# Seven block products for eight in the first products of three experts

## The chip, the cores and the metric

The kernel runs on one core of a Trainium2 chip. The engines of that core are TensorE (PE in the profile; PEld is its weight load), VectorE (DVE), ScalarE (ACT), GpSimd (POOL) and the queue engine SyncE (SP), which starts the DMA transfers. SBUF is the core's main memory, PSUM the memory of eight banks into which TensorE writes its sums. The metric is the time of one execution on the device, in microseconds (us): the median of three runs.

## The reference

Three networks follow each other on 1152 tokens (2 batches of 576) of 512 features.

```python
# attention: 8 heads of 64, a window of 128 keys back, a bias per head
scores = where(mask, scale * q @ k.T + bias, -1e9); attn = softmax(scores); x = attn @ v
# network one: four experts, F = 1024
p = domain_probs / domain_probs.sum(-1)
for e in range(4):
    out += p[:, e:e+1] * (maximum(x @ w1[e], 0) @ w2[e])
# network two, F = 2048
h = maximum(x @ w_in, 0);  y = (h * h) @ w_out
```

## The kernel before

**Three products for one.** Each fp32 operand is kept as a rounded high part and the rest (names that end in h and l). A product is three matmuls into one sum: high by high, and high by rest both ways.

**Items.** Network two is cut into two halves of 1024 hidden columns, which count as experts 4 and 5 (E = 4 is the number of real experts, NE = 6 of both). The tokens of an expert are cut into three chunks of 384 (CHUNKS); expert 0, which runs beside the attention, has four chunks (256, 256, 256, 384: CHUNKS0). An item (e, ch, f) is a chunk and one of the eight tiles of 128 hidden columns. Its first product (gemm1_mm, matmuls on L757) sums over four tiles of 128 features: 4 x 3 = 12 matmuls of 384 columns into one "work" bank. ScalarE writes the relu's high part (hh, L772), VectorE the rest (hl, L773); in network two VectorE squares first (L779) and POOL writes the rest (L781). The second product (gemm2, L791) is 3 token tiles x 3 = 9 matmuls of 512 columns into three "y" banks, and runs LAG = 3 items behind. After the eighth f of a chunk VectorE adds the three y banks to y in SBUF, times the expert's probability (L805 for expert 0, L809 for experts 1 to 3).

**Weights.** They come in quarters g of 256 hidden columns: a w1 tile of 128 x 4 x 256 and a w2 tile of 128 x 2 x 512. For experts 1 to 3 ScalarE writes the high part (L273) and POOL the rest (L275). The weights of network two come as 64-bit floats that VectorE takes apart in integer steps (split64: L199, L202, L206, L210, and the rest L275), with ScalarE copies between (L195, L273).

**What sets the order.** A planner (Plan, with costs and due times) orders the attention together with expert 0's first three chunks. From expert 0's last chunk on (item N1 = 24) a loop at the end of the function writes the items out one after another. Each engine runs its instructions in the order in which that loop issues them. Small closures prepare the weights of what comes later; pace gives each item its number of them. Between experts 3 and 4, y is turned into the x of network two by TensorE transpositions (to_x2, L823, four of 128 x 128 for each token tile), with the high part on ScalarE (L827) and the rest on VectorE (L828); one token tile every second item.

Of the kernel before, what the change touches and what calls it, by code (L numbers as in the profile page):

```python
# [10 lines left out]
I32 = mybir.dt.int32  # L11
# [12 lines left out]
CHUNKS = [(0, 384), (384, 384), (768, 384)]  # L24

# [103 lines left out]
def kernel(  # L129
# [34 lines left out]
    hp = ctx.enter_context(tc.tile_pool(name="hp", bufs=4))  # L164
# [17 lines left out]
    def split64(raw, n, t):  # L182

        lo, hi = raw[:, :, 0], raw[:, :, 1]
        stt = nc.vector.scalar_tensor_tensor

        def begin():
            t["a"] = late["w"].tile([P, n], F32, tag="wfull", name="wfull", bufs=3)
            t["b"] = late["w"].tile([P, n], I32, tag="wtmp", name="wtmp", bufs=2)
            t["ai"] = t["a"].bitcast(I32)
            nc.scalar.activation(out=t["a"], in_=hi.bitcast(F32), func=ACTF.Abs, scale=65536.0)  # L195

        return [
            begin,
            lambda: nc.vector.tensor_scalar(  # L199
                out=t["b"], in0=hi, scalar1=-(1 << 31), scalar2=None, op0=ALU.bitwise_and  # L200
            ),
            lambda: nc.vector.tensor_scalar(  # L202
                out=t["a"], in0=t["a"], scalar1=8053063680.0, scalar2=2.0,
                op0=ALU.min, op1=ALU.max,
            ),
            lambda: stt(  # L206
                out=t["b"], in0=lo, scalar=29, in1=t["b"],
                op0=ALU.logical_shift_right, op1=ALU.bitwise_or,
            ),
            lambda: stt(  # L210
                out=t["ai"], in0=t["ai"], scalar=3, in1=t["b"],
                op0=ALU.logical_shift_left, op1=ALU.bitwise_or,
            ),
        ]
# [10 lines left out]
    free = []  # L225
    raws = {}
# [31 lines left out]

    def w_ops(i):
# [4 lines left out]
        parts = (w1t, w2t)[k]  # L264

# [50 lines left out]
    def chunks(e):  # L316
# [4 lines left out]
        rq=3, rk=3, rv=2, qh=2, ql=2, khl=2, vp=2, sc=2, tp=2, ts=5, st=5, pt=2, work=2, y=2, h=4  # L321
# [440 lines left out]

    def h_tiles(n):
        return [hp.tile([P, 3 * P], F32R, tag=t, name=t)[:, 0:n] for t in ("hh", "hl")]

    def gemm1(e, ch, f):
# [9 lines left out]
        else:  # L776
            r = late["w"].tile([P, n], F32, tag="r", name="r", bufs=2)
# [18 lines left out]
    def evac(e, ch, tiles):  # L796
        c0, cn = chunks(e)[ch]
# [21 lines left out]
    def to_x2(ch, i):  # L819
        nt = CHUNKS[ch][0] // P + i  # L820
# [23 lines left out]
    items = [(e, ch, f) for e in range(NE) for ch in range(len(chunks(e))) for f in range(FT)]  # L844
    first_item = [items.index((e, 0, 0)) for e in range(NE)]
# [6 lines left out]
    def run_x2():  # L852
        if x2todo:
            what = x2todo.pop(0)
            if what:
                to_x2(*what)

    def flush_one():
        e, ch, f, h = pend.pop(0)
        if f == 0:  # L860
            ys[e, ch] = [
                (i, ps_tile("y", [P, DM], "yacc")) for i in range(chunks(e)[ch][1] // P)
            ]
        gemm2(e, ch, f, h, ys[e, ch])
        w_done(w2t, e, ch, f)
        if f == FT - 1:
            evac(e, ch, ys.pop((e, ch)))
            if e == E - 1:
                x2todo.extend(x for i in range(CHUNKS[ch][1] // P) for x in (None, (ch, i)))

    def attn_close():
        if "w" not in late:
            actx.close()
            late["w"] = ctx.enter_context(tc.tile_pool(name="wlate", bufs=1))
            add_buffers(late["w"], 12)
# [4 lines left out]
    def loads(limit=len(order), ahead=2 * NQ):  # L880

        while wnext["load"] < limit:
            i = wnext["load"]
            wait = i - wnext["ops"] + bool(bg)
            wide = order[i][0] >= E
            if wait >= ahead or (wide and "w" not in late):
                return
            narrow = sum(order[p][0] < E for p in range(i - wait, i))
            if len(free) < 2 + narrow + (2 if wide else 1):
                return  # L890
            w_load(i)
            wnext["load"] += 1

    def pace(it):

        i = wnext["ops"]
        if i == len(order):
            return len(bg)
        pe = order[i][0]
        if pe == 0:  # L900
            return 1
        left = max(first_item[pe] - it - 1, 1)
        todo = ((pe + 1) * PER - i) * (1 if pe < E else 14) + len(bg)
        return -(-todo // left)

    def bg_some(n):
        for _ in range(n):
            if not bg and wnext["ops"] < wnext["load"]:
                w_start()
            bg_run(1)  # L910

    def w_done(parts, e, ch, f):
        if ch == len(chunks(e)) - 1 and f % FTQ == FTQ - 1:
# [190 lines left out]
    attn_close()  # L1104

    for it, (e, ch, f) in list(enumerate(items))[N1:]:
        loads()
        need = 2 * (e * NQ + f // FTQ) + 1
        if need not in ready:
            bg_run()  # L1110
            while wnext["ops"] <= need:
                loads()
                w_start()
                bg_run()
            while carry:
                carry.pop(0)()
        run_x2()
        quota = pace(it)
        pend.append((e, ch, f, gemm1(e, ch, f)))
        w_done(w1t, e, ch, f)  # L1120
        bg_some(quota - quota // 2)
        if len(pend) > LAG:
            flush_one()
        bg_some(quota // 2)

# [37 lines left out]
```

## Time and profile before

| | us |
|---|---|
| median of three runs | 703.45 (703.31 to 703.74) |
| the profiled execution | 703.92, of which the span is 702.1 |
| TensorE busy | 691.1 |
| VectorE busy | 301.7 |
| ScalarE busy | 260.8 |
| POOL busy | 204.7 |

Busy times are sums over a group's instructions; matmuls overlap in their pipeline, so the spacing of starts, not the duration of one, says what a matmul costs in a row. The chain is followed back from the last instruction to what released it; a piece of it on TensorE is time in which nothing else held the program.

### The profile page before, as it was taken

How to read it: one execution, taken by the hardware profiler on the slowest of the kernel's cores; microseconds unless marked ns; L12 is line 12 of the kernel's file. 1: busy time of each engine (PE TensorE's matmuls, PEld its weight loads, DVE VectorE, ACT ScalarE, POOL GpSimd, SP SyncE). 2: the span in 40 equal slices, each digit the busy share in tenths (PEclk: the TensorE clock that was granted, in tenths of full speed). 3: DMA queues.
4: the chain of work that ended last, by engine and by line, in shares of the span. 5: the costliest groups of instructions: out<-in, count | busy, mean ns of one | idle time of the engine just before them, and what ended most of it. 6: DMA issues, size and time to landing. Idle time of an engine off the chain costs nothing.

```text
span 702.1 us, 9945 instructions
## 1 busy us (share of the span) xinstructions
PE 691.1 (98%) x3848; PEld 624.1 (89%) x3848; DVE 301.7 (43%) x706; ACT 260.8 (37%) x601; POOL 204.7 (29%) x212
## 2 busy tenths in 40 slices
PE   8998999999999999999999999999999999999997
PEld 7787998889999999999999999999999999999996
DVE  4688867732121212122123656527776627112121
ACT  5886777533331113311112222314445434322221
POOL 4898745408550004510011000000222222222221
PEclk7899999999999999999999999999999999999999
DMA  8753221233400011300005400036300020001011
GB/s 211 204 165 91 79 73 44 71 104 107 150 31 1 0 31 61 119 31 1 0 31 186 175 0 1 31 122 212 117 0 1 31 91 0 1 1 45 1 46 45
DMA packets 37103, 47.58 MB, mean 68 GB/s; under 512 B 3392, under 2 KB 25408, under 8 KB 37056
## 3 DMA queue, kind: packets, MB, share of 16 engines
q1 hardware_dynamic: 37056, 46.95, 21.5%
q8 instruction: 30, 0.49, 0.3%
q14 instruction: 17, 0.14, 0.1%
HBM read 44.58 MB, written 2.36 MB: 67 GB/s over the span
## 4 chain that ended last, share of the span: by engine, by line
PE 91%; POOL 1%; issue 0%; DVE 0%
PE yacc L791 42%; PE hps L757 42%; PE xps L578 3%; PE tp L680 2%; PE sc L632 1%; PE xtp L823 1%; POOL vl L349 0%; POOL ql L349 0%; POOL wl L349 0%; POOL ts L668 0%; DVE y L815 0%
## 5 line engine op out<-in xcount | busy, mean ns | idle before, releaser
L757 PE MATMUL hps<-xh,wh 128*128 128x384 f32 (+1 forms) x608 | 202.1, 332 | 0.6 <-DVE hl L1062 0.6
L757 PE MATMUL hps<-xh,wl 128*128 128x384 f32 (+1 forms) x608 | 200.2, 329 | 0.0
L757 PE MATMUL hps<-xl,wh 128*128 128x384 f32 (+1 forms) x608 | 199.7, 328 | 0.0
L791 PE MATMUL yacc<-wh,hl 128*128 128x512 f32 x432 | 170.8, 395 | 0.0
L791 PE MATMUL yacc<-wl,hh 128*128 128x512 f32 x432 | 170.5, 395 | 0.0
L791 PE MATMUL yacc<-wh,hh 128*128 128x512 f32 x432 | 169.2, 392 | 0.0
L773 DVE SCALAR_TENSOR_TENSOR hl<-hps,hh 128x384 fp32r<-128x384 f32 x80 | 44.6, 557 | 227.7 <-ACT hh L772 227.6
L772 ACT ACTIVATE hh<-hps 128x384 fp32r<-128x384 f32 x80 | 39.4, 492 | 245.1 <-PE hps L757 245.1
L781 POOL TENSOR_TENSOR hl<-r,hh 128x384 fp32r<-128x384 f32 x48 | 50.8, 1058 | 266.0 <-ACT hh L780 262.5
L757 PEld LDWEIGHTS hps<-xh,wh 128*128 128x128 f32 x608 | 115.3, 190 | 6.7 <-DVE hl L1062 0.8
L757 PEld LDWEIGHTS hps<-xl,wh 128*128 128x128 f32 x608 | 115.2, 189 | 5.3
L757 PEld LDWEIGHTS hps<-xh,wl 128*128 128x128 f32 x608 | 114.9, 189 | 0.0
L275 POOL TENSOR_TENSOR wl<-wraw,wh 128x1024 fp32r<-128x1024 f32 x24 | 57.2, 2390 | 173.0 <-ACT wh L273 165.7
L791 PEld LDWEIGHTS yacc<-wh,hl 128*128 128x128 f32 x432 | 81.0, 187 | 17.5
L791 PEld LDWEIGHTS yacc<-wl,hh 128*128 128x128 f32 x432 | 81.1, 188 | 13.3
L791 PEld LDWEIGHTS yacc<-wh,hh 128*128 128x128 f32 x432 | 81.2, 188 | 12.8
L779 DVE TENSOR_TENSOR r<-hps,r 128x384 f32<-128x384 f32 x48 | 26.7, 556 | 102.6 <-ACT r L778 102.6
L778 ACT ACTIVATE r<-hps 128x384 f32<-128x384 f32 x48 | 23.6, 491 | 92.0 <-PE hps L757 92.0
L668 POOL TENSOR_SCALAR ts<-ts,st 128x256 f32<-128x256 f32 (+2 forms) x80 | 38.8, 498 | 33.4 <-DVE st L663 18.5
L653 ACT ACTIVATE ts<-ts,st 128x256 f32<-128x256 f32 (+2 forms) x80 | 37.1, 466 | 9.0 <-DVE st L644 8.9
L780 ACT ACTIVATE hh<-r 128x384 fp32r<-128x384 f32 x48 | 25.2, 526 | 35.6 <-DVE r L779 35.6
L275 DVE TENSOR_TENSOR wl<-wfull,wh 128x512 fp32r<-128x512 f32 x32 | 28.3, 884 | 6.4 <-ACT wh L273 6.4
(76 smaller groups left out, 686.5 us busy)
## 6 DMA issues: line engine op xcount, KB each, us to landing
wraw<-in_w_dram SPq DMA_DIRECT2D x32, 512.0 KB, 3.8
wraw<-in_w_in_dram SPq DMA_DIRECT2D x16, 512.0 KB, 4.3
wraw<-in_w_out_dram SPq DMA_DIRECT2D x16, 512.0 KB, 4.2
rq<-in_qT_dram SPq DMA_DIRECT2D x8, 256.0 KB, 6.7
out_dram<-y SPq DMA_DIRECT2D x8, 256.0 KB, 2.1
rk<-in_kT_dram SPq DMA_DIRECT2D x8, 192.0 KB, 6.6
rv<-in_v_dram SPq DMA_DIRECT2D x8, 192.0 KB, 2.6
rq<-in_qT_dram SPq DMA_DIRECT2D x8, 192.0 KB, 2.5
```

Of the source, the lines that this page charges most:

```text
L275: eng.tensor_tensor(out=lo[:, ks, :], in0=full, in1=f32(hi[:, ks, :]), op=ALU.subtract)
L578: nc.tensor.matmul(out=xps[0:rows, o0:o0 + w], lhsT=l_, rhs=r_, start=start, stop=(i == len(mm) - 1 and a == 0 and l_ is wl_), skip_group_ ...
L653: nc.scalar.activation(out=ts[0:n, g, :], in_=ts[0:n, g, :], func=ACTF.Exp, bias=st[0:n, 0, g:g + 1], scale=-1.0, accum_out=st[0:n, 1, g:g ...
L668: nc.gpsimd.tensor_scalar(out=ts[0:n, g, :], in0=ts[0:n, g, :], scalar1=st[0:n, 2, g:g + 1], scalar2=1.0, op0=ALU.mult, op1=ALU.mult,)
L757: nc.tensor.matmul(out=ps, lhsT=l_[:, k, cs], rhs=r_[:, k, cols], start=(k == 0 and r_ is xh and l_ is wh and not second), stop=(k == KT - ...
L772: nc.scalar.activation(out=hh, in_=ps, func=ACTF.Relu)
L773: nc.vector.scalar_tensor_tensor(out=hl, in0=ps, scalar=0.0, in1=f32(hh), op0=ALU.max, op1=ALU.subtract)
L778: nc.scalar.activation(out=r, in_=ps, func=ACTF.Relu)
L779: nc.vector.tensor_tensor(out=r, in0=ps, in1=r, op=ALU.mult)
L780: nc.scalar.activation(out=hh, in_=r, func=ACTF.Copy)
L781: nc.gpsimd.tensor_tensor(out=hl, in0=r, in1=f32(hh), op=ALU.subtract)
L791: nc.tensor.matmul(out=y, lhsT=l_[:, ns], rhs=r_[:, fo, :], start=(f == 0 and j == 0), stop=(f == FT - 1 and j == 2),)
```

## The change

**Seven products.** For experts 1 to 3 the tokens are cut into pairs of two equal halves: pair A is tokens 0 to 511 (2 x 256), pair B tokens 512 to 1151 (2 x 320). With the 512 features in two halves and a quarter's 256 hidden columns in two halves, the first product of a pair and a quarter is a 2 x 2 by 2 x 2 block product, and seven block products with sums of blocks (Winograd's form) take the place of eight. The item is now (e, pair, quarter): 7 products x 2 feature tiles x 3 = 42 matmuls (gemm1_pair, L891) of 256 or 320 columns, into three banks pa, pb, pc. In the order of the code the seven are a11·b11 (pa), s2·t2 (pb), s1·t1 (pc), a12·b21 (on top in pa), s3·t3 (on top in pb, after VectorE has read u2 = pb + p1), s4·b22 (on top in pc, after ScalarE has copied p5), a22·m4 (on top in pb, after u3 = pb + p1). VectorE makes the sums u2, u3, c12, c21 and the four rests hl, ScalarE the copies p1, p5 and the four high parts, POOL c22.

**Sums of weights.** For each quarter POOL forms the four sums s1 to s4 (wsum, four adds, L281) and the rests la and ls (L402); ScalarE the high parts ha (L287) and hs (L306). These closures stand in w_forms.

**Sums of x.** VectorE forms t1, t2, m4 and t3 for each pair, high part and rest (x_forms, adds on L846, ScalarE copies on L864), in six steps. The loop issues pair A's steps behind the first six items of expert 0's last chunk, and pair B's three behind each of the first two paired items. Expert 1's items come in the order (A, quarter 0), (A, 1), (B, 0), (B, 1), (A, 2), (A, 3), (B, 2), (B, 3), as for the other two.

**Second products.** gemm2_pair (L940) is 4 or 5 token tiles x 2 x 3 matmuls of 512 columns, one item behind. y is added after every two quarters (L989): 54 adds for 27.

**Into network two.** The transpositions (now L1002, with xh on ScalarE and xl on VectorE, L1007) of pair A's four token tiles stand right behind the first products of the last paired item; the other five are spread over every second item as before. The buffers for weights are cut anew (18 + 6, and 8 more once network two begins), rk of the attention has two slots for three, and loads, pace and the look-ahead are rewritten to go by time.

```diff
+PAIRS = [(0, 256), (512, 320)]
...
+        return [
+            begin,
+            lambda: (part(0, 4, raw[:, :, 0:P]), part(4, 2, a22)),
+            lambda: add(0, lambda: a21, lambda: a22, ALU.add),
+            lambda: add(2, s(0), lambda: a11, ALU.subtract),
+            lambda: add(4, lambda: a11, lambda: a21, ALU.subtract),
+            lambda: add(6, lambda: a12, s(2), ALU.subtract),
+            lambda: part_lo(0, 4, raw[:, :, 0:P]),
+            lambda: (part_lo(4, 2, a22), free.append(buf)),
+            lambda: nc.scalar.activation(out=t["hs"][0], in_=t["s"], func=ACTF.Copy),
+            done,
+        ]
...
-        rq=3, rk=3, rv=2, qh=2, ql=2, khl=2, vp=2, sc=2, tp=2, ts=5, st=5, pt=2, work=2, y=2, h=4
+        rq=3, rk=2, rv=2, qh=2, ql=2, khl=2, vp=2, sc=2, tp=2, ts=5, st=5, pt=2, work=2, y=2, h=4
...
+        t1 = make(0, "t1", ((h12, h11), ((l12, plus), (l11, sub))))
+        t2 = make(1, "t2", ((h22, lambda: place(0)), ((l22, plus),)))
+        m4 = make(0, "m4", ((h21, lambda: place(1)), ((l21, plus),)))
+        t3 = make(1, "t3", ((h22, h12), ((l22, plus), (l12, sub))))
+        return [
+            t1[0], t1[1] + t2[0], t1[2] + t2[1] + m4[0], t2[2] + m4[1] + t3[0], m4[2] + t3[1],
+            t3[2],
+        ]
...
+        pa, pb, pc = (ps_tile("work", [P, n], "hps") for _ in range(3))
+        mm(pa, a11, f["b11"], True, False)
+        nc.scalar.activation(out=p1, in_=pa, func=ACTF.Copy)
+        mm(pb, s2, f["t2"], True, False)
+        add(u2, pb, p1)
+        mm(pc, s1, f["t1"], True, False)
+        nc.scalar.activation(out=p5, in_=pc, func=ACTF.Copy)
+        mm(pa, a12, f["b21"], False, True)
+        relu(0, 0, pa)
+        mm(pb, s3, f["t3"], False, False)
+        add(u3, pb, p1)
+        mm(pc, s4, f["b22"], False, True)
+        add(c12, pc, u2)
+        relu(0, 1, c12)
+        mm(pb, a22, f["m4"], False, True)
+        add(c21, pb, p1)
+        relu(1, 0, c21)
+        nc.gpsimd.tensor_tensor(out=c22, in0=u3, in1=p5, op=ALU.add)
+        relu(1, 1, c22)
...
+    xbg = x_forms(0, "DVE") + [[]] * 2 + x_forms(1, "DVE")
...
         quota = pace(it)
-        pend.append((e, ch, f, gemm1(e, ch, f)))
+        if paired(e):
+            h = gemm1_pair(e, ch, f)
+            if it == items.index((E, 0, 0)) - 1:
+                run_x2(4)
+                x2wait = it + 2
...
         w_done(w1t, e, ch, f)
+        x_step()
+        if paired(e):
+            x_step()
         bg_some(quota - quota // 2)
-        if len(pend) > LAG:
+        if len(pend) > (1 if paired(e) else LAG):
             flush_one()
+        if paired(e):
+            x_step()
         bg_some(quota // 2)
```

How the instructions stand on three engines, before and now. First VectorE where expert 1 begins: in the kernel before, the rests hl (L773) of items and the y adds of chunks.

```order
L773 SCALAR_TENSOR_TENSOR hl<-hps,hh 128x384 x3
L805 TENSOR_SCALAR y<-yacc,pt 128x512 x2
L773 SCALAR_TENSOR_TENSOR hl<-hps,hh 128x384 x8
L805 TENSOR_SCALAR y<-yacc,pt 128x512 x3
L773 SCALAR_TENSOR_TENSOR hl<-hps,hh 128x384 x8
```

The same place in the changed kernel, from the last rest of item (1, A, 0) to the sums of item (1, A, 1); fxwork is the work tile of x_forms, lt the rest of t1, u and c the sums of the seven products (L901).

```order
380 L906 SCALAR_TENSOR_TENSOR hmem<-c_2542,hmem 128x256
381 L985 TENSOR_SCALAR y<-yacc,pt 128x512 x3
382 L846 TENSOR_TENSOR fxwork<-xh 128x640
383 L846 TENSOR_TENSOR fxwork<-fxwork,xl 128x640 x2
384 L846 TENSOR_TENSOR fxwork<-xh,fxwork 128x640
385 L846 TENSOR_TENSOR fxwork<-fxwork,xl 128x640
386 L846 TENSOR_TENSOR lt_2637<-fxwork,ht_2636 128x640
387 L846 TENSOR_TENSOR fxwork<-xh,fxwork 128x640
388 L846 TENSOR_TENSOR fxwork<-fxwork,xl 128x640
389 L901 TENSOR_TENSOR u_2670<-hps,p_2668 128x256
390 L906 SCALAR_TENSOR_TENSOR hmem<-hps,hmem 128x256
391 L901 TENSOR_TENSOR u_2671<-hps,p_2668 128x256
```

Three y adds and eight operations of pair B's sums now stand ahead of u2 (row 389), on which the fifth block product waits.

Next ScalarE at that place. Before, a copy of weights stands between the high parts of two items.

```order
186 L772 ACTIVATE hh<-hps 128x384
187 L273 ACTIVATE wh<-wraw 128x1024
188 L772 ACTIVATE hh<-hps 128x384
189 L273 ACTIVATE wh<-wraw 128x1024
190 L772 ACTIVATE hh<-hps 128x384
```

Now, from the last high part of item (1, A, 0) to p1 (L915) of item (1, A, 1):

```order
198 L905 ACTIVATE hmem<-c_2542 128x256
199 L864 ACTIVATE ht_2636<-fxwork 128x640
200 L306 ACTIVATE hs<-wsum 128x1024
201 L326 ACTIVATE wh<-wraw 128x1024
202 L864 ACTIVATE ht_2642<-fxwork 128x640
203 L287 ACTIVATE ha<-wraw 128x512
204 L287 ACTIVATE ha<-wraw 128x256
205 L915 ACTIVATE p_2668<-hps 128x256
```

The copy hs (row 200), the high part of quarter 1's weight sums, stands behind the copy of pair B's t1 (row 199), which waits for the first three adds on VectorE; and p1 stands behind the copy of pair B's t2 (row 202).

Last VectorE at the end of expert 3. Before, between two rests of expert 3 (L773), a few steps of the split of network two's weights:

```order
472 L773 SCALAR_TENSOR_TENSOR hl<-hps,hh 128x384
473 L210 SCALAR_TENSOR_TENSOR wfull<-wfull,wtmp 128x512
474 L199 TENSOR_SCALAR wtmp<-wraw_4711 128x512
475 L202 TENSOR_SCALAR wfull<-wfull 128x512
476 L773 SCALAR_TENSOR_TENSOR hl<-hps,hh 128x384
```

Now, from the y adds of (A, quarters 2 and 3) to the first sum of item (3, B, 3); wroom is the split's work tile.

```order
614 L989 SCALAR_TENSOR_TENSOR y<-yacc,pt,y 128x512 x4
615 L203 TENSOR_SCALAR wroom<-wraw_5087 128x512
616 L206 TENSOR_SCALAR wroom<-wroom 128x512
617 L210 SCALAR_TENSOR_TENSOR wroom<-wraw_5087,wroom 128x512
618 L328 TENSOR_TENSOR wl<-wroom,wh 128x512
619 L214 SCALAR_TENSOR_TENSOR wroom<-wroom 128x512
620 L203 TENSOR_SCALAR wroom<-wraw_5089 128x512
621 L901 TENSOR_TENSOR u_5141<-hps,p_5139 128x320
```

Six steps of the split and four y adds stand ahead of u2 (row 621), where before two or three steps stood between two rests that nothing on TensorE waited for at once.

## Rows read from the trace of the kernel before

**Rows 1.** page, busy time, share of the span and instructions of each engine
```profile
PE 691.1 (98%) x3848; PEld 624.1 (89%) x3848; DVE 301.7 (43%) x706; ACT 260.8 (37%) x601; POOL 204.7 (29%) x212
```

**Rows 2.** chain of waits: start us, us, what
```profile
by line: PE yacc L791 42.0%; PE hps L757 41.7%; PE xps L578 3.2%; PE tp L680 1.6%; PE sc L632 1.4%; PE xtp L823 0.6%; POOL vl L349 0.3%; POOL ql L349 0.3%; POOL wl L349 0.2%; POOL ts L668 0.2%; issue 0.1%; DVE y L815 0.1%
...
301.03 2.08 PE yacc L791 x9
303.11 2.10 PE hps L757 x12
```

**Rows 3.** windows: us, busy of PE, PEld, DVE, ACT, POOL, granted clock, DMA share, GB/s
```profile
36.00:42.00 6.00, 5.83 (x40) 5.35 (x38) 4.57 (x19) 6.00 (x18) 6.00 (x8) 0.72 0.39 123
...
154.00:186.00 32.00, 32.00 (x164) 29.16 (x163) 5.86 (x11) 12.47 (x17) 19.64 (x9) 1.00 0.45 150
186.00:488.00 302.00, 302.00 (x1527) 273.75 (x1526) 97.94 (x180) 68.94 (x123) 37.60 (x16) 1.00 0.18 60
```

**Rows 4.** timeline of PE, 26 to 42: start us, us, engine, line, operation
```profile
28.37 0.28 PE L757 MATMUL hps<-xh,wh 128*128 128x256 f32 x1
...
30.41 0.28 PE L757 MATMUL hps<-xh,wl 128*128 128x256 f32 x1
...
38.03 0.41 PE L757 MATMUL hps<-xh,wh 128*128 128x256 f32 x1
...
39.95 0.36 PE L757 MATMUL hps<-xh,wh 128*128 128x256 f32 x1
```

**Rows 5.** timeline of VectorE, 398 to 412
```profile
398.46 0.69 DVE L275 TENSOR_TENSOR wl<-wfull,wh 128x512 fp32r<-128x512 f32 x1
399.07 0.68 DVE L210 SCALAR_TENSOR_TENSOR wfull<-wfull,wtmp 128x512 int32<-128x512 int32 x1
399.67 2.06 DVE L809 SCALAR_TENSOR_TENSOR y<-yacc,pt,y 128x512 f32<-128x512 f32 x3
...
402.55 0.42 DVE L202 TENSOR_SCALAR wfull<-wfull 128x512 f32<-128x512 f32 x1
402.88 0.68 DVE L206 SCALAR_TENSOR_TENSOR wtmp<-wraw,wtmp 128x512 int32<-128x512 int32 x1
```

**Rows 6.** ScalarE by line and shape: xcount | busy us, mean ns | idle before
```profile
L273 ACT ACTIVATE wh<-wraw 128x1024 fp32r<-128x1024 f32 x24 | 25.2, 1052 | 0.0
...
L273 ACT ACTIVATE wh<-wfull 128x512 fp32r<-128x512 f32 x32 | 19.9, 621 | 2.5 <-DVE wfull L210 2.5
...
L1059 ACT ACTIVATE hh<-hps 128x256 fp32r<-128x256 f32 x24 | 9.0, 378 | 7.3 <-PE hps L757 6.6 <-DVE st L644 0.5
```

**Rows 7.** POOL by line and shape
```profile
L275 POOL TENSOR_TENSOR wl<-wraw,wh 128x1024 fp32r<-128x1024 f32 x24 | 57.2, 2390 | 173.0 <-ACT wh L273 165.7 <-issue 7.4
...
L349 POOL TENSOR_TENSOR wl<-wraw,wh 128x512 fp32r<-128x512 f32 x12 | 15.7, 1318 | 0.9 <-ACT wh L343 0.9
...
L349 POOL TENSOR_TENSOR vl<-rv,vh 128x256 fp32r<-128x256 f32 x4 | 3.0, 743 | 3.5 <-ACT vh L343 3.5
```

**Rows 8.** VectorE by line and shape
```profile
L275 DVE TENSOR_TENSOR wl<-wfull,wh 128x512 fp32r<-128x512 f32 x32 | 28.3, 884 | 6.4 <-ACT wh L273 6.4
...
L1062 DVE SCALAR_TENSOR_TENSOR hl<-hps,hh 128x256 fp32r<-128x256 f32 x24 | 9.9, 414 | 4.0 <-ACT hh L1059 3.0 <-PE hps L757 0.9
```

**Rows 9.** timeline of ScalarE, 300 to 304
```profile
301.07 0.49 ACT L772 ACTIVATE hh<-hps 128x384 fp32r<-128x384 f32 x1 [3.69 <-PE hps L757]
```

**Rows 10.** chain of waits, 480 to 495
```profile
480.67 0.44 PE xtp L823 x4
```

**Rows 11.** timeline of VectorE, 490 to 497
```profile
493.71 0.68 DVE L206 SCALAR_TENSOR_TENSOR wtmp<-wraw,wtmp 128x512 int32<-128x512 int32 x1
494.31 1.50 DVE L275 TENSOR_TENSOR wl<-wfull,wh 128x512 fp32r<-128x512 f32 x1
```

**Rows 12.** timeline of POOL, 490 to 500
```profile
493.76 1.51 POOL L781 TENSOR_TENSOR hl<-r,hh 128x384 fp32r<-128x384 f32 x1 [117.62 <-ACT hh L780]
497.94 1.01 POOL L781 TENSOR_TENSOR hl<-r,hh 128x384 fp32r<-128x384 f32 x1 [2.68 <-ACT hh L780]
```

## What the change will do to the time

> **What bounds the kernel now.** I read the page's busy times first: TensorE works 691.1 of 702.1 us, VectorE 301.7 [rows 1]. Then the chain of waits: the matmuls of L791 and L757 hold 83.7% of it, and around 300 us it is nothing but their alternation, 2.10 us for twelve matmuls of 384 columns and 2.08 us for nine of 512 [rows 2]. The windows say the same of the whole stretch that the change touches: TensorE is busy 302.00 of 302 us from 186 to 488, while VectorE works 98, ScalarE 69 and POOL 38 [rows 3]. So there a matmul less is time less, until one of the other three engines comes late. From here it is TensorE's saving against the waits that the new sums bring.
>
> **What is saved.** The spacing of starts is the price of a matmul in a row: 2.10 / 12 = 0.175 us for 384 columns [rows 2] and (30.41 − 28.37) / 17 = 0.120 us for 256 at full clock [rows 4]. 320 columns lie halfway, so by these two 0.1475 us (an estimate). A quarter's first products cost 72 x 0.175 = 12.60 us before; now 42 x 0.120 + 42 x 0.1475 = 5.04 + 6.20 = 11.24 us: 1.36 us less. Three experts of four quarters make 12 x 1.36 = 16.3 us. It is 11% and not an eighth, since the shorter matmuls cost more per column. The second products stay 54 matmuls of 512 columns for each quarter, at 2.08 / 9 = 0.231 us. An item of pair A is then 5.04 + 24 x 0.231 = 10.6 us of TensorE, of pair B 6.20 + 30 x 0.231 = 13.1 us. If 320 columns cost 0.003 us more or less than halfway, the saving moves by 1.5 us either way.
>
> **Where expert 1 begins (7.6 us lost).** VectorE's order puts eight sums of pair B ahead of u2 of item (1, A, 1), and ScalarE's puts hs of that item behind the copy of t1. Let 0 be the end of the second products before that item, when its first products should start. VectorE takes three y adds, which follow each other at 0.66 us (2.06 us for three [rows 5]) and end about 0.9 us after the last bank. A sum over 512 elements starts 0.60 us after the one before (399.07 to 399.67) and lasts 0.69 us alone [rows 5]; one over 640, each waiting for the one before, I put at 0.85 us, 0.69 x 640 / 512. Three of them end at 3.4. The copy of t1 takes 0.75 us (0.62 for 512 [rows 6], scaled) to 4.15; hs over 1024 elements 1.05 us [rows 6] to 5.2; then POOL's rest ls over 1024, 2.39 us [rows 7], to 7.6. TensorE needs ls at the ninth matmul, 8 x 0.120 = 0.96 us after 0. That is a wait of 6.6 us. u2 comes after all eight sums, and a sum that runs beside POOL's long rest is held: with that it ends at about 10.4, while TensorE, going on from 7.6, wants it at 7.6 + 16 x 0.120 = 9.5. That adds about 1: I take 7.6 us. The ends: 5.4 if sums overlap as at 0.60 us, 9.5 if POOL's rest itself is held by a sum.
>
> **The clock after that wait (1.0 us).** From 38.03 to 39.95 nine matmuls of 256 columns started 0.213 us apart, in a window whose granted clock was 0.72, against 0.120 us at full clock [rows 3, 4]: the lower of the two levels (1.2 and 2.4 GHz). That stretch followed pauses of TensorE below 1 us each. After a pause of 7 us I expect the like: the 16 matmuls or so that ran at the lower level there (37 to 40) lost 0.093 us each, 1.5 us in all. Part of it would lie under the wait for u2; I take 1.0, ends 0 and 2.
>
> **Pair B's last sums (0.5 us).** Five more sums of 640 stand between the last rest of (1, A, 1) and u2 of (1, B, 0), 5 x 0.85 = 4.3 us behind a tail that ends some 2.3 us after the first products (two more relus at 0.38 [rows 6], rests at 0.41 [rows 8]). The second products in between last 24 x 0.231 = 5.5 us and the first three block products 18 x 0.1475 = 2.7 us: 8.2 us of cover for 6.6 us of work, plus the copy of t3 and hs ahead of p1. By this it just holds: 0; if POOL holds the sums for one of its rests, 2.4. I take 0.5.
>
> **Expert 3's first item (1.3 us).** ScalarE's order there is the tail of (2, B, 3), a copy wh, ha, hs, another wh that waits for the last use of its buffer on TensorE, then p1. hs waits for four adds on POOL that stand behind a rest of 2.39 us. From the end of the first products of (2, B, 3): tail 1.7, wh 1.05, rest 2.39, four adds of 256 at 0.65 (0.74 [rows 7] in a busy stretch), hs 1.05, wh 1.05, p1 and u2 0.4 each: 10.9 us. The cover is 30 x 0.231 = 6.9 plus 24 x 0.120 = 2.9, 9.8 us. Late by 1.1 to 1.6; ends 0 and 3.
>
> **Into network two (4.9 us).** VectorE splits 64-bit weights in steps of 0.33 (402.55 to 402.88) or 0.60 us [rows 5], with a ScalarE copy of 0.62 us [rows 6] between. Before (3, A, 3): five y adds end 0.9 after the second products, then 0.33 + 0.60 + 0.65 + 0.60 + 0.60 + 0.33 = 3.1 us, then u2 0.45: 4.45, needed at 24 x 0.120 = 2.88: 1.6 us late. Before (3, B, 3): four y adds and the six steps of the fence, 0.9 + 3.6 + 0.45 = 4.95 against 24 x 0.1475 = 3.5: 1.4 late. Then the transpositions: there are three banks, so the fourth waits until VectorE has taken the rest from the first. That follows the item's tail: 2.5 + 0.7 = 3.2 us, against 3 x 0.44 [rows 10] = 1.3: 1.9 late. Sum 4.9. The rests of the split took 0.88 us on average, not 0.69 [rows 5, 8], as often as POOL or ScalarE came between: upper end 9, lower end 2. ScalarE's start 0.2 us behind the last matmul (a high part starts at 301.07 [rows 9]) is in each of these.
>
> **Hidden.** Pair A's sums lie in 154 to 186, where VectorE works 5.9 us of 32 [rows 3]; 14 sums of 0.69 go there. The y adds double, 27 x 0.74 = 20 us, but TensorE has other banks meanwhile. POOL's work per quarter is 2.39 x 2 + 4 x 0.74 + 1.3 + 0.74 + two c22 of some 0.8 = 11.4 us of 23.7 [rows 7]. The attention's order, with one slot less for rk, I put at 0, ends −1 and +2.
>
> **The sum.** −16.3 + 7.6 + 1.0 + 0.5 + 1.3 + 4.9 = −1.0 us on the profiled execution's 703.92: 702.9. The median lies 0.47 us below it: 702.4.
>
> A rule of the Trainium skill speaks against the change. First the rows: a VectorE rest of 0.69 us alone took 1.50 at 494.31, and POOL's 1.01 us rest took 1.51 from 493.76, just as long as the two would take one after the other with the step at 493.71 [rows 5, 11, 12]. "SBUF — State Buffer" (section on who interferes with whom) says that a VectorE instruction with two SBUF inputs and a GpSimd instruction that reads SBUF exclude each other for a whole instruction. The rows agree. By it every sum of x, and each rest of c12, c21 and c22, can stand behind a 2.39 us rest; with nothing held, (1, A, 1) would lose 6.6 us for 7.6 and the second rival below would go.
>
> **Rivals.** *The waits are half of what I count* (0.22). The ends add to 5.4 + 0 + 0 + 0 + 2 = 7.4 us, so −8.9: 694.6. For it: pace spreads the closures, and TensorE idles nowhere now. Against: the orders of the three engines are fixed, and the sums stand there ahead of u2.
>
> *POOL holds VectorE in every item: slower* (0.28). The place is the tail of each paired item: c22 and the rests from SBUF stand behind or beside POOL's rests of 2.39 us [rows 7, 12]. The y adds end 0.9 us after the second products and u2 needs about 1 more, so the spare time to u2 is about 1 us in pair A. It decides once VectorE is held longer than that in the regular items. At 0.5 us in the mean for the 24 items, 24 x 0.5 = 12 us: −1.0 + 12 = 714.4. Against: the item's tail has 5.5 us of second products to pass in.
>
> *The saving is not made* (0.02): a 320-column matmul costs as much as one of 384. Then 42 x 0.0275 x 12 = 13.9 us more: 716. The rows of 256 and 384 speak against it.
>
> **How the numbers follow.** Forecast 0.48: saving and waits nearly cancel, own range 697 to 708; of that 0.21 lies under 702.0, 0.17 within 0.2% (1.4 us, about what a measurement here can tell from no change) and 0.10 above. With the rivals: faster 0.21 + 0.22 = 0.43, same 0.17, slower 0.10 + 0.30 = 0.40. The range reaches to 692 (all waits at their low ends, the saving 1.5 larger and the attention 1 us shorter: 703.45 − 8.9 − 2.5) and to 713, short of the slower rival's point.
>
> **What would show it.** The spacing of L891 should read 0.120 and 0.147 us; a regular pair of items 23.7 us. TensorE should idle 6 to 9 us just before the ninth matmul of item (1, A, 1), released by POOL's ls, then by VectorE; and 1 to 2 us twice at the end of expert 3, released by VectorE's u2, and once at the fourth transposition. Idle time before s3·t3 in most items would speak for the slower rival; a gap of under 3 us at (1, A, 1) for the faster one. Wrong altogether if the chain leaves TensorE for long in the regular items.

## The result and the profile after

The changed kernel takes 708.28 us (708.17 to 710.11), the kernel before 703.6 in the same runs: a ratio of 1.007 (95% interval 1.0052 to 1.0089), so 0.7% slower. The forecast was 702.4, no change. The profiled execution spans 706.5 us for 702.1.

The page, as in [rows 1]:

```profile
PE 677.6 (96%) x3992; PEld 610.4 (86%) x3992; DVE 413.3 (58%) x880; ACT 298.6 (42%) x700; POOL 295.9 (42%) x314
```

TensorE now works 13.5 us less than before and the span is 4.4 us longer: the columns were saved, and TensorE waits for more than it saved. Windows, as in [rows 3] (us; busy of PE, PEld, DVE, ACT, POOL; granted clock; DMA share; GB/s):

```profile
154.00:186.00 32.00, 32.00 (x168) 29.25 (x167) 20.95 (x24) 10.17 (x19) 16.93 (x14) 1.00 0.29 99
186.00:488.00 302.00, 287.39 (x1654) 259.40 (x1653) 173.57 (x310) 103.93 (x214) 126.29 (x106) 0.98 0.17 56
488.00:706.00 218.00, 212.46 (x1066) 190.50 (x1064) 110.57 (x180) 79.20 (x154) 52.08 (x48) 1.00 0.15 53
```

In 186 to 488, where TensorE had no idle time at all, it now idles 14.6 us, while VectorE's work rose from 98 to 174 us and POOL's from 38 to 126. From 154 to 186 VectorE took pair A's sums (20.95 us for 5.86) without a cost to TensorE. The chain of waits over regular items (start us, us, what) reads as forecast:

```profile
243.22 5.11 PE hps L891 x42
248.33 6.83 PE yacc L940 x30
...
384.62 2.16 PE hps L891 x18
...
388.61 1.46 PE hps L891 x10
```

42 matmuls take 5.11 us in pair A (0.122 each) and 6.16 in pair B (0.147), 24 and 30 second products 5.47 and 6.83. The last two rows are item (3, A, 0), broken off between 386.8 and 388.6. TensorE's waits stand in its timeline as a bracket at the end of a row (idle time before, and who ended it). Behind the first paired item these are the ones above 1 us:

```profile
201.15 0.58 PE L891 MATMUL hps<-ht,hs 128*128 128x256 f32 x1 [4.30 <-ACT hs L306]
...
204.10 0.58 PE L891 MATMUL hps<-ht,ls 128*128 128x256 f32 x1 [2.15 <-POOL ls L402]
...
220.99 0.41 PE L891 MATMUL hps<-xh,ha 128*128 128x320 f32 x1 [1.72 <-ACT p L915]
...
388.61 0.38 PE L891 MATMUL hps<-xh,ha 128*128 128x256 f32 x1 [1.84 <-ACT p L915]
...
450.08 0.39 PE L891 MATMUL hps<-xh,hs 128*128 128x256 f32 x1 [1.42 <-DVE u L901]
...
475.06 0.41 PE L891 MATMUL hps<-xh,hs 128*128 128x320 f32 x1 [1.91 <-DVE u L901]
...
519.47 0.45 PE L810 MATMUL hps<-xh,wh 128*128 128x384 f32 x1 [1.34 <-ACT wh L326]
```

From the start of an item's first products to the start of the second products behind them, five of the 24 paired items take longer than their 5.11 or 6.16 us: (1, A, 1) 15.03, (1, B, 0) 8.14, (3, A, 0) 7.22, (3, A, 3) 6.76 and (3, B, 3) 9.87. That is 9.9 + 2.0 + 2.1 + 1.7 + 3.7 = 19.4 us. The four transpositions take 3.47 us (479.34 to 482.81) where 4 x 0.44 would do: 1.7 more. From the first item of network two to the end of its matmuls it is 206.2 us for an even run of 48 x 4.18 + 5 x 0.44 = 202.8: 3.4 more.

### The profile page after: what moved, and what is told of

Same layout as the page of the kernel before. It is cut to its first block, busy times and chain, and to the rows that moved or that the text cites. A ratio compares the mean times of both kernels' runs of the same rounds, so it can differ in the third digit from the quotient of the medians.

```text
span 706.5 us, 10701 instructions
## 1 busy us (share of the span) xinstructions
PE 677.6 (96%) x3992; PEld 610.4 (86%) x3992; DVE 413.3 (58%) x880; ACT 298.6 (42%) x700; POOL 295.9 (42%) x314
## 4 chain that ended last, share of the span: by engine, by line
PE 87%; DVE 6%; ACT 2%; POOL 2%; issue 1%; SPq 1%; DMA 1%; ACTq 0%; POOLq 0%
PE yacc L940 20%; PE yacc L971 20%; PE hps L810 20%; PE hps L891 18%; PE xps L631 4%; PE tp L733 2%; PE sc L685 2%; DVE fxwork L846 1%; DVE wl L328 1%; DMA wraw<-in_w_dram 1%; SPq L1164 1%; POOL wl L402 1%; DVE wroom L214 1%; ACT wh L326 0%; PE xps L613 0%
## 5 line engine op out<-in xcount | busy, mean ns | idle before, releaser
L971 PE MATMUL yacc<-wh,hmem 128*128 128x512 f32 x432 | 147.5, 394 | 0.0
L940 PE MATMUL yacc<-wh,hmem 128*128 128x512 f32 x432 | 137.1, 390 | 0.0
L810 PE MATMUL hps<-xh,wh 128*128 128x384 f32 (+1 forms) x320 | 104.0, 325 | 1.6 <-ACT wh L326 1.3
L810 PE MATMUL hps<-xh,wl 128*128 128x384 f32 (+1 forms) x320 | 102.8, 321 | 0.6 <-DVE wl L328 0.6
L810 PE MATMUL hps<-xl,wh 128*128 128x384 f32 (+1 forms) x320 | 102.3, 320 | 0.0
L940 PEld LDWEIGHTS yacc<-wh,hmem 128*128 128x128 f32 x432 | 81.1, 188 | 16.4
L971 PEld LDWEIGHTS yacc<-wh,hmem 128*128 128x128 f32 x432 | 81.2, 188 | 15.3
L971 PE MATMUL yacc<-wl,hmem 128*128 128x512 f32 x216 | 85.1, 394 | 0.0
L940 PE MATMUL yacc<-wl,hmem 128*128 128x512 f32 x216 | 84.3, 390 | 0.0
L810 PEld LDWEIGHTS hps<-xh,wh 128*128 128x128 f32 x320 | 60.3, 189 | 4.9 <-ACT wh L326 1.7
L810 PEld LDWEIGHTS hps<-xl,wh 128*128 128x128 f32 x320 | 60.3, 188 | 2.3
L810 PEld LDWEIGHTS hps<-xh,wl 128*128 128x128 f32 x320 | 60.2, 188 | 1.2 <-DVE wl L328 1.2
L906 DVE SCALAR_TENSOR_TENSOR hmem<-c,hmem 128x256 fp32r<-128x256 f32 (+1 forms) x72 | 45.7, 661 | 24.5 <-ACT hmem L905 24.5
L901 DVE TENSOR_TENSOR u<-hps,p 128x256 f32<-128x256 f32 (+1 forms) x48 | 21.8, 455 | 58.0 <-PE hps L891 49.2
L940 PEld LDWEIGHTS yacc<-wl,hmem 128*128 128x128 f32 x216 | 40.6, 188 | 7.7
L971 PEld LDWEIGHTS yacc<-wl,hmem 128*128 128x128 f32 x216 | 40.6, 188 | 6.5
```

Source lines behind the costliest of these rows:

```text
L810: nc.tensor.matmul(out=ps, lhsT=l_[:, k, cs], rhs=r_[:, k, cols], start=(k == 0 and r_ is xh and l_ is wh and not second), stop=(k == KT - ...
L901: nc.vector.tensor_tensor(out=out, in0=x, in1=y, op=ALU.add)
L906: nc.vector.scalar_tensor_tensor(out=hl, in0=src, scalar=0.0, in1=f32(hh), op0=ALU.max, op1=ALU.subtract)
L940: nc.tensor.matmul(out=y, lhsT=l_[:, ns], rhs=r_[:, fo, :], start=(first and fo == 0 and j == 0), stop=(last and fo == FTQ - 1 and j == 2),)
L971: nc.tensor.matmul(out=y, lhsT=l_[:, ns], rhs=r_[:, fo, :], start=(f == 0 and j == 0), stop=(f == FT - 1 and j == 2),)
```

## Where expert 1 begins

VectorE, from the y adds to u2 (start us, us, line, operation):

```profile
194.82 2.11 DVE L985 TENSOR_SCALAR y<-yacc,pt 128x512 f32<-128x512 f32 x3 [2.69 <-PE yacc L971]
...
201.87 2.86 DVE L846 TENSOR_TENSOR fxwork<-xh,fxwork 128x640 f32<-128x640 f32 x1
204.76 2.88 DVE L846 TENSOR_TENSOR fxwork<-fxwork,xl 128x640 f32<-128x640 f32 x1
207.56 0.41 DVE L901 TENSOR_TENSOR u<-hps,p 128x256 f32<-128x256 f32 x1
```

ScalarE's copy of t1 and the copy hs behind it:

```profile
199.41 0.74 ACT L864 ACTIVATE ht<-fxwork 128x640 fp32r<-128x640 f32 x1 [7.76 <-DVE fxwork L846]
200.06 1.04 ACT L306 ACTIVATE hs<-wsum 128x1024 fp32r<-128x1024 f32 x1
```

And POOL:

```profile
201.24 2.81 POOL L402 TENSOR_TENSOR ls<-wsum,hs 128x1024 fp32r<-128x1024 f32 x1 [11.40 <-ACT hs L306]
204.01 2.95 POOL L328 TENSOR_TENSOR wl<-wraw,wh 128x1024 fp32r<-128x1024 f32 x1
206.92 1.30 POOL L281 TENSOR_TENSOR wsum<-wraw 128x256 f32<-128x256 f32 x1
```

The order did what the prediction said: hs behind the copy of t1, ls behind hs, u2 behind eight sums. What it put too small is in the last two sums: 2.86 and 2.88 us for 0.82. Each was held by a POOL rest of 1024 elements (201.24 and 204.01) until that ended. The prediction counted one such hold; the second, by the rest of the w2 quarter, it did not count.

The 9.9 us of item (1, A, 1) have two parts. Its fifth block product, the first that needs u2, starts at 208.03, 12.05 us after the item's start, where 24 matmuls take 2.9: 9.1 us. The 18 matmuls behind that start take 2.98 us for 2.19, because the first six still run at the lower clock (granted clock 0.50 from 204.1 to 209.4): 0.8 us.

```profile
208.03 0.58 PE L891 MATMUL hps<-xh,hs 128*128 128x256 f32 x1
```

## Experiments

**Sums ahead of the second products.** To tell the order from the holds and from a second wait that only stood behind the first.

```diff
+        turn = paired(e) and not paired((pend or [(e,)])[0][0])
+        if turn:
+            for _ in range(3):
+                x_step()
             while pend:
                 flush_one()
...
```

> Pair B's first three steps of sums are issued ahead of expert 0's last second products and y adds, the rest as in the changed kernel. Theory 1 (the order on VectorE and ScalarE makes the wait at the first products of item (1, A, 1)): the sums then run from about 192 to 198.7 us beside 6 us of second products, hs and ls follow from about 195, the item takes about 8 us for 15.0 and the time falls by about 7 us to 701. Rival 2 (POOL's rests hold VectorE's sums wherever they stand): the sums of 0.8 us still take up to 2.9 us each, the item stays above 13 us and the time above 706. Rival 3 (the wait only hides another that stands behind it): the item shortens, but a later item lengthens by as much, and the time stays within 1.5 us of 708.3.

Measured: 705.42 us, ratio 1.0033 to before (1.0020 to 1.0046). Item (1, A, 1) takes 11.4 us for 15.0. VectorE, the first sum and the last:

```profile
191.78 0.82 DVE L846 TENSOR_TENSOR fxwork<-xh 128x640 f32<-128x640 f32 x1
...
197.66 0.82 DVE L846 TENSOR_TENSOR fxwork<-fxwork,xl 128x640 f32<-128x640 f32 x1
```

All eight sums pass in 6.7 us, none held, since POOL's ls came later. The place was right, the gain less than half of what I expected: hs still stood behind pair B's copies, so hs cost 1.24 us, ls began at 197.89 and its wait was 2.45. The other 2.6 us over 5.11 are the lower clock: the granted clock from 201 to 205 is 0.50, and 20 matmuls behind the wait for ls start 0.213 us apart. The fifth block product, which needs u2, starts among them (204.33) and waits for nothing:

```profile
201.34 0.41 PE L891 MATMUL hps<-lt,hs 128*128 128x256 f32 x1
...
204.33 0.41 PE L891 MATMUL hps<-xh,hs 128*128 128x256 f32 x1
```

**Weight sums first too.** As before, with this line ahead of the x steps:

```diff
+            want(2 * (e * NQ + g + 1))
```

> As the run before, and the remaining weight closures of quarter 1 (hs, ls) are issued ahead of the sums. Theory 1: TensorE no longer waits at the ninth matmul (ls is ready by about 196.5 us), but the y adds end at about 200.7, so u2 still costs about 2 us; item about 7.3 us, time about 700.5. Rival 2: ls of 2.4 us now runs beside the sums, holds them, and u2 comes later than in the run before: no gain over it, or a loss of 1 to 2 us.

Measured: 702.77 us, ratio 1.0005 (0.9987 to 1.0024): level with the kernel before. The wait for ls is gone, and so is (1, B, 0)'s (6.35 us for 8.14). But the sums now run beside ls:

```profile
192.30 3.77 DVE L846 TENSOR_TENSOR fxwork<-fxwork,xl 128x640 f32<-128x640 f32 x2
```

Two sums take 3.77 us for 1.69: one was held for the rest of ls, which began at 192.13. p1 and u2 come 3.0 and 1.0 us late and the item takes 11.2 us, not 7.3; 2.2 of it are the lower clock behind the wait for u2 (granted clock 0.50 from 202.6 to 206.6). So both theories hold a part: order made the wait, and POOL's hold of one sum added some 2 us in the second.

**Closures ahead of the y adds.** For the waits at the end of expert 3.

```diff
-        bg_some(quota - quota // 2)
+        bg_some(quota if paired(e) else quota - quota // 2)
...
-        bg_some(quota // 2)
+        bg_some(0 if paired(e) else quota // 2)
```

> Paired items issue all their weight closures ahead of the second products and the y adds, not half of them behind; sums of x as in the changed kernel. Theory 1 (in front of network two u2 is late because the split's steps stand behind the y adds): items (3, A, 3) and (3, B, 3) lose their 1.4 and 1.9 us waits and the pause's low clock (1.5 us), time about 704. Rival (VectorE is simply full there, 37 of 51 us busy): the waits move to the rests or to network two's first items, time within 1 us of 708.3.

Measured: 709.14 us, ratio 1.0082 (1.0066 to 1.0099). (3, A, 3) waits 1.09 us for 1.42, (3, B, 3) 1.91 as before, and (3, A, 0) takes 9.6 us for 7.2, so nothing is gained. My reason fell: moving the split's steps ahead of the y adds leaves as many instructions between the last rest and u2.

**Transpositions behind the second products.**

```diff
-                run_x2(4)
...
         if len(pend) > (1 if paired(e) else LAG):
             flush_one()
+        if x2wait == it + 2:
+            run_x2(4)
```

> The four transpositions of pair A stand behind the second products of item (3, B, 2), which follow the last first products, not ahead of them. Theory 1: they find VectorE free and lose no time (1.7 us less), and the 4.3 us that VectorE idles at 489 to 494 behind the y adds is used; time about 706 to 706.6. Rival (network two's weights are late anyway): the 1.7 us comes back as longer waits in network two's first items, time 708 to 708.5.

Measured: 709.49 us, ratio 1.0088 (1.0069 to 1.0107), not told apart from the changed kernel's. The fourth transposition waits 0.54 us for 0.98, and network two's first items wait as before. Alone it gives nothing that shows.

**Sums in the idle slots.** Six steps of pair B begin at the sixth item of expert 0's last chunk; two of them stand ahead of the second products.

```diff
-    xbg = x_forms(0, "DVE") + [[]] * 2 + x_forms(1, "DVE")
+    xbg = x_forms(0, "DVE") + x_forms(1, "DVE")
...
+        if (e, f) == (0, 0):
+            x_step()
...
+        if turn:
+            want(2 * (e * NQ + g + 1))
+            for _ in range(2):
+                x_step()
...
```

> Pair B's sums start two items earlier (pair A's first two steps share one item of expert 0's last chunk, and three steps of pair B follow in that chunk), two steps and quarter 1's last weight closures stand ahead of the last second products of expert 0, one behind item (1, A, 1). Theory 1 (order alone): VectorE ends the y adds by about 197 us, p1 and u2 of (1, A, 1) come in time, the item takes 5.1 to 6 us for 15.0 and item (1, B, 0) loses its 1.7 us wait or part of it; time about 697.5 to 699.5 against 703 of the kernel before, 9 to 11 us under the changed kernel. Rival 2 (VectorE and POOL hold each other, so more work in 154 to 186 makes those items late): the last items of expert 0's chunk or item (1, A, 0) gain waits of 2 us or more, and the time stays above 701.

Measured: 699.0 us, ratio 0.9956 (0.9937 to 0.9974): 0.4% faster than the kernel before. Of its waits up to the end of expert 3, the first two:

```profile
200.20 0.39 PE L891 MATMUL hps<-xh,ha 128*128 128x256 f32 x1 [2.05 <-ACT p L915]
...
378.88 0.39 PE L891 MATMUL hps<-xh,ha 128*128 128x256 f32 x1 [1.82 <-ACT p L915]
```

Item (1, A, 1) takes 7.4 us for 15.0 and (1, B, 0) 6.16, no wait. The 2.05 us that stay are p1's: one sum is held again (2.91 us), and copies of weights stand ahead of p1 on ScalarE.

**Closures inside the products.** The second half of an item's closures is issued inside the next item's gemm1_pair.

```diff
         nc.scalar.activation(out=p5, in_=pc, func=ACTF.Copy)
+        mid(1)
...
         add(u3, pb, p1)
+        mid(None)
...
-        bg_some(quota // 2)
+        if paired(e):
+            owed.append(quota // 2)
```

> The second half of each paired item's weight closures is issued inside the next item's first products: one behind u2 and p5, the others behind u3, not between the y adds and u2. Sums of x as in the changed kernel. Theory 1 (place): (3, A, 3) and (3, B, 3) start their fifth block product in time (1.4 and 1.9 us of waits and 1.5 us at the lower clock gone), and p1 of (3, A, 0) no longer stands behind a copy that waits for a buffer (1.8 gone): 5 to 6 us less than the changed kernel, about 702.5. Rival (VectorE is full there): the rests come later and the waits reappear at the transpositions and in network two, gain under 2 us.

Measured: 707.12 us, ratio 1.0054 (1.0034 to 1.0074). The waits of (3, A, 0) and (3, B, 3) are gone, (1, B, 0)'s falls from 1.72 to 0.70. New or left, above 1 us:

```profile
449.62 0.39 PE L891 MATMUL hps<-xh,hs 128*128 128x256 f32 x1 [1.60 <-DVE u L901]
...
479.14 0.66 PE L1004 MATMUL xtp<-ident,y 128*128 128x128 f32 x4 [3.38 <-DVE c L901]
```

The rival was right for this kernel: the time that (3, B, 3) no longer waits comes back at the transpositions (3.38 us, behind c21 on VectorE), which stand right behind it. The wait of 1.34 us in network two's seventh item is gone here.

**All three edits together.**

> The two edits before together, and the four transpositions behind the second products that follow the last first products. If the places were the cause, the gains add: 10 + 5 + 1 us less than the changed kernel, 691 to 694, 1.3 to 1.7% under the kernel before; what is left are network two's first items (3.4 us). If VectorE's amount of work is the cause at the end of expert 3, about 697 to 698.

Measured: 693.29 us, ratio 0.9862 (0.9844 to 0.9880): 1.4% faster than the kernel before and 15.0 us under the changed kernel, as forecast by place and not the 697 to 698 of the other theory. Measured alone the first two edits gave 9.3 and 1.2 us and the third nothing that shows; 4.5 us come only from having them together. Most of that stands at the transpositions: behind the second products they take 2.99 us, in the run before 6.81, since the work that they waited for there finds cover. The three longest waits that stay:

```profile
200.03 0.39 PE L891 MATMUL hps<-xh,ha 128*128 128x256 f32 x1 [2.06 <-ACT p L915]
...
440.71 0.39 PE L891 MATMUL hps<-xh,hs 128*128 128x256 f32 x1 [1.60 <-DVE u L901]
...
475.68 0.66 PE L1004 MATMUL xtp<-ident,y 128*128 128x128 f32 x4 [1.11 <-DVE xl L1009]
```

**The kernel before with two slots for rk.**

```diff
-        rq=3, rk=3, rv=2, qh=2, ql=2, khl=2, vp=2, sc=2, tp=2, ts=5, st=5, pt=2, work=2, y=2, h=4
+        rq=3, rk=2, rv=2, qh=2, ql=2, khl=2, vp=2, sc=2, tp=2, ts=5, st=5, pt=2, work=2, y=2, h=4
```

> The kernel before with two slots for rk in place of three, nothing else. In the changed kernel expert 0's last chunk starts 1.0 us earlier (153.52 for 154.53). If the other order of the attention does that, this kernel starts the chunk at about 153.5 too and is 1 us faster than before; if not, the chunk starts at 154.5 and the time is within 0.5 us of before.

Measured: 702.84 us, ratio 1.0000 (0.9991 to 1.0010); the chunk starts at 154.97. Two slots alone do nothing. In the profiles the changed kernel and eight of its nine versions reach expert 1 between 183.5 and 184.9 us, the last one at 186.0; the kernel before and this run are there at 185.7 and 186.2. Whether the 1.0 us is a gain of the change's other edits or a spread from one execution to the next, one profile of each can't tell, and its cause was not looked for.

**TensorE kept busy through the wait.** Does the low clock after the wait have a price of its own? 18 more matmuls of the same kind stand ahead of the item's ninth matmul.

```diff
...
         mm(pa, a11, f["b11"], True, False)
+        if (e, ch, g) == (1, 0, 1):
+            for _ in range(34):
+                nc.tensor.matmul(
+                    out=pc, lhsT=xh[:, 0, 0:P], rhs=xh[:, 0, 0:n], start=True, stop=True,
+                    skip_group_check=True,
+                )
...
```

> The changed kernel, with 34 matmuls of 256 columns into the bank pc (which the next product overwrites) put ahead of the second block product of item (1, A, 1), and 18 more ahead of its third matmul: 4.1 and 2.2 us of work for TensorE inside waits of 4.30 and 2.15 us, so nothing is meant to come later for them. If the low clock after the wait costs on its own, the matmuls that follow keep 0.120 us for 0.213 and the item ends up to 2 us earlier, 706.5 to 707. If the low clock lies wholly under the wait for u2 (which VectorE gives at 208.0), u2's wait grows by as much and the time stays at 708.3.

Measured: 708.55 us, ratio 1.0092 (1.0064 to 1.0119). TensorE around the item's waits, and one matmul after them:

```profile
200.22 0.39 PE L897 MATMUL hps<-ht,hs 128*128 128x256 f32 x1 [0.22 <-ACT hs L306]
...
203.21 0.39 PE L897 MATMUL hps<-ht,ls 128*128 128x256 f32 x1 [0.33 <-POOL ls L402]
...
207.16 0.39 PE L897 MATMUL hps<-xh,hs 128*128 128x256 f32 x1 [1.77 <-DVE u L907]
...
208.31 0.42 PE L897 MATMUL hps<-xh,ls 128*128 128x256 f32 x1
```

The waits shrink to 0.22 and 0.33 us and the clock holds, so TensorE reaches the fifth block product 1.4 us earlier in the item, and there waits 1.77 us for u2. u2 comes 12.1 us after the item's start in both. So in the changed kernel the low clock ahead of u2 lay under VectorE's delay and cost nothing. What it cost behind u2, 0.8 us, this run could not take away: here the clock fell behind the 1.77 us pause, at 208, and the 18 matmuls behind u2 take 3.29 us, the item 15.4. Where no matmul waits for u2 the low clock has its full price: 2.6 us in the same item of *Sums ahead of the second products*.

**All weight closures behind u3.** For p1's last wait, and for the slower rival of the prediction.

```diff
-        bg_some(quota - quota // 2)
+        ahead = 0 if paired(e) and e < E - 1 else quota - quota // 2
+        bg_some(ahead)
...
-            owed.append(quota // 2)
+            owed.append(quota - ahead)
```

> The version with all three edits, and for experts 1 and 2 all closures of the weights (not the second half) stand inside the next item's first products, behind u2, p5 and u3. Theory 1 (place on ScalarE): p1 of (1, A, 1) no longer stands behind copies of weights, its 2.06 us wait goes, time about 691. Rival 2 (POOL's queue decides): c22 now stands behind rests of 2.4 us on POOL, the last rest of each pair comes late and holds VectorE in front of u2 in many items of experts 1 and 2: waits of 1 us or more in most items, time 697 or more.

Measured: 699.99 us, ratio 0.9954 (0.9936 to 0.9973), 6.7 us above the version with all three; 1.7 of it is there before expert 1 begins. p1's wait falls to 0.28 us, but u2 then comes 1.02 us late, and the item takes 6.9 us for 7.4. Item (3, A, 1) takes 10.2 us for 5.4, and its chain of waits is the rival's:

```profile
389.50 2.54 POOL ls L402
392.05 0.89 POOL c L932
...
393.75 3.38 DVE y L991 x5
397.13 0.34 DVE u L901
...
397.51 3.77 PE hps L891 x18
```

POOL's rest stands ahead of c22, c22 holds up the last rest, that the y adds, they u2. It happened in full in this one item, not in most as the rival said; those of experts 1 and 2 behind (1, A, 1) lose 1.0 us at most.

## Why the prediction was wrong

The saving was right. First products were put at 16.3 us less; 12 x (5.11 + 6.16) = 135.2 against 12 x 12.60 = 151.2 is 16.0. The second products gave 2.2 us that were put at nothing: in runs of 24 or 30 one costs 5.47 / 24 = 0.228 us, in runs of nine 0.231 [rows 2]. The regular items run at 23.6 us for a pair of items, 23.7 forecast, with no wait: the slower rival did not happen in this kernel, and the saving is made.

The waits came where they were named (of the 6.6 us at the ninth matmul of (1, A, 1) 4.30 fell to the seventh, which already needs hs), but three terms were 1.5 to 2.3 us too low, one 0.8, and one was left out. Forecast 15.3 us in all; measured 19.4 + 1.7 + 3.4 = 24.5. With the savings of 18.2 that makes +6.3 us; from the start of expert 0's last chunk to the last sum it is 549.2 us for 543.8, +5.4, so 0.9 stays unassigned. The second products' 2.2 us, put at nothing, hid a part of the error by luck.

- *Expert 1's first items*: 7.6 (waits), 1.0 (clock) and 0.5 (pair B's last sums) forecast; 9.1, 0.8 and 2.0 measured. The step that failed is the one that ends in "that adds about 1". By its own terms u2 comes at 10.4 us: 0.9, eight sums of 0.85 and 0.45 for u2 leave room for one hold by POOL, 2.2 us. Two came, 2.04 us each, and u2 came at 12.0. The w2 quarter's rest stands right behind ls on POOL, and its copy stood in the fence on ScalarE (row 201). In (1, B, 0) the hold that the prediction named as its upper end came as well: two rests and a sum beside POOL's rests la (from 213.29) took 3.54 us for 1.58, and the copy of t3, hs and p1 behind them came late.

```profile
212.84 2.19 DVE L906 SCALAR_TENSOR_TENSOR hmem<-c,hmem 128x256 fp32r<-128x256 f32 x2 [0.48 <-ACT hmem L905]
214.96 1.35 DVE L846 TENSOR_TENSOR lt<-fxwork,ht 128x640 fp32r<-128x640 f32 x1
```

- *Expert 3's first item*: 1.3 forecast, 2.1 measured. The steps were right, and 0.4 us longer than put: hs waited for POOL's adds, the copy wh and p1 followed. The cover was counted 0.7 us too long: TensorE stopped at the fourth block product, which writes on in the bank that p1 copies, so 18 matmuls of cover stood there, 2.2 us, and not the 24, 2.9 us, that were counted up to u2.
- *(3, A, 3), (3, B, 3) and the transpositions*: 1.6, 1.4, 1.9 forecast; 1.7, 3.7, 1.7 measured. u2 of (3, B, 3) was 1.91 us late by

```profile
466.60 0.42 DVE L203 TENSOR_SCALAR wroom<-wraw 128x512 int32<-128x512 int32 x1
...
469.08 2.72 DVE L989 SCALAR_TENSOR_TENSOR y<-yacc,pt,y 128x512 f32<-128x512 f32 x4
471.71 0.42 DVE L203 TENSOR_SCALAR wroom<-wraw 128x512 int32<-128x512 int32 x1
...
474.52 0.48 DVE L901 TENSOR_TENSOR u<-hps,p 128x320 f32<-128x320 f32 x1
```

(the first of five split steps behind the tail; the y adds, which start late behind those steps; six more steps; u2). The y adds ended 2.3 us after the second products and not 0.9, because the steps in front of them had not let them start. The rest of the 3.7 is mostly the lower clock behind this wait (granted clock 0.50 from 476.2 to 479.1), 0.266 us for 320 columns instead of 0.147, from the sixth matmul on; the prediction had no term for it here:

```profile
476.21 0.47 PE L891 MATMUL hps<-xh,hs 128*128 128x320 f32 x1
476.47 0.47 PE L891 MATMUL hps<-xl,hs 128*128 128x320 f32 x1
```

- *Network two's first items*: 0 forecast, 3.4 measured: a term that was left out. Its longest wait, 1.34 us at 519, is in the seventh item, for weights that the split had not finished. VectorE idles 4.32 us in front of the y adds of the last pair, with steps of the split behind them:

```profile
489.04 0.42 DVE L206 TENSOR_SCALAR wroom<-wroom 128x512 f32<-128x512 f32 x1
493.77 3.47 DVE L989 SCALAR_TENSOR_TENSOR y<-yacc,pt,y 128x512 f32<-128x512 f32 x5 [4.32 <-PE yacc L940]
```

That this idle time makes the split late is near at hand, but two runs speak against it. With the transpositions behind the second products VectorE idles 0.31 us in front of these y adds (and 2.61 in front of the transpositions' rests), and the wait in network two stays (1.36 us):

```profile
491.44 3.47 DVE L989 SCALAR_TENSOR_TENSOR y<-yacc,pt,y 128x512 f32<-128x512 f32 x5 [0.31 <-PE yacc L940]
```

With the closures inside the products VectorE idles 4.23 us, in front of a step of the split, and the wait is gone:

```profile
491.32 0.69 DVE L328 TENSOR_TENSOR wl<-wroom,wh 128x512 fp32r<-128x512 f32 x1 [4.23 <-PE yacc L942]
```

Network two takes 204.3 us there and with all three edits, for 206.2. So the new place of the closures takes the wait away; which step of the split comes late in the changed kernel stays open.

The range 692 to 713 held the time, but by the wrong terms: the forecast called the gain eaten, and it was overdrawn by a left-out term (3.4 us), by one hold counted where two came (1.5), by a hold that was taken at a small share (1.5) and by the late u2 of (3, B, 3) with its low clock (2.3). The versions that beat the kernel before keep the seven products; the cause of the loss is the order around them and the holds that this order brings, shown by changing the order: 15.0 us.

The rule of the Trainium skill that the prediction quotes ("SBUF — State Buffer", who interferes with whom: a VectorE instruction with two SBUF inputs and a GpSimd instruction that reads SBUF exclude each other) agrees with this trace, in [rows 11, 12] and in the sum of 2.86 us beside the rest of 2.81 us above; u2, with one input in PSUM, took its 0.41 us at 207.56 beside POOL's sum from 206.92 on, and was not held.

## What to carry to other kernels

When a change saves time on the bound engine by adding work to others, list for each of them what stands in its queue ahead of the first instruction that the bound engine waits for, at every place where the rhythm changes: a new stage, its first and last item. Count every long instruction on an engine that can hold another as a full hold. Move the new work into the slots in which that engine idles anyway, ahead of instructions that wait for the bound engine and not behind them; here the three moves together were worth some 15 us, nearly as much as the saving itself.

## What the runs showed of the hardware

A sum of 0.82 us with two SBUF inputs that met a POOL rest (2.39 us alone) took up to 2.9 us, its own time plus what was left of POOL's: 2.86 and 2.88 us in the changed kernel, 2.91 with the sums in the idle slots. The clock fell after some waits of TensorE and not after others of the same length: behind the 1.9 us wait of (3, B, 3) the item took 9.85 to 9.87 us in three versions, and 8.31 to 8.34 in four others. What decides it was not found.
